# Two of sixteen x tiles transposed through DRAM and VectorE, in a transformer block whose scheduler is set and drawn anew

## The chip, the cores and the metric

The kernel runs on one core of a Trainium2 chip. The core has five engines, each with its own instruction queue that is worked off in order: TensorE (PE) for matmuls, VectorE (DVE), ScalarE (ACT), GpSimd (POOL), and SyncE (SP), which issues the DMAs here. Engines meet only at semaphores. The metric is the device time of one launch in microseconds (us). Before the change it is 519.75 us, the median of three runs (519.67 to 520.14).

## The reference

A pre-norm transformer block on 2048 rows of width 512, in float32: sliding dilated attention with 32 heads of width 16 (each row looks at itself and at 7 rows before it at steps of two), then an MLP of width 1792 with a squared ReLU.

```python
h = x + _A_ref(_layernorm(x), A_wqkv, A_wo)
h2 = h + _B_ref(_layernorm(h), B_w1, B_b1, B_w2, B_b2)
# _A_ref:
qkv = (x @ wqkv).reshape(B, S, 3, H, Dh).transpose(2, 0, 3, 1, 4)
idx = pos[:, None] - (jnp.arange(8) * 2)[None, :]
logits = jnp.where(idx >= 0, einsum("bhsd,bhswd->bhsw", q, kg) * Dh ** -0.5, -1e9)
o = einsum("bhsw,bhswd->bhsd", softmax(logits), vg) @ wo
# _B_ref:
r = relu(h @ w1 + b1); out = (r * r) @ w2 + b2
```

## The kernel before

Matmuls run on a split of every operand into a high half (rounded to the fast matmul type, `fp32r`) and a low half (the rest): three products, high by high, high by low, low by high, give the float32 accuracy. So each operand costs a cast (`hi`, line 322, ACT) and a subtraction (`lo`, line 327, POOL or DVE). In the trace the halves are called xh and xl (of x), oh and ol (of the attention output o), big_h and big_l (of wqkv, later of the normalised h), rh and rl (of the MLP's hidden rows).

The 2048 rows are 16 tiles of 128; four tiles make a unit, u = 0 to 3. The stages:

- **qkv.** Tiles 0 to 3 run first, in pieces of 384 columns (`qkv_first`, product at line 457 with result mm, copied to y by ACT at line 508) while wqkv is still arriving. Its 16 pieces wraw are loaded (line 488), cast (big_h<-wraw) and subtracted one by one. Tiles 4 to 15 run in pairs: `x_chain(t)` (lines 826 to 835) loads x, normalises it on ACT (lines 378 to 390), transposes it and splits it, and `qkv` multiplies. The results go to DRAM (qkv_d).
- **The transpose of x**, two ways. `pe_turn` (line 401) transposes four 128x128 blocks on PE into PSUM (tr); ACT casts xh from there and DVE subtracts xl, and only then is that PSUM buffer free. `turned` (lines 437 to 446) writes the rows to DRAM (t_d), reads them back in another order (back), and DVE transposes 32x32 blocks (`turn`, line 428); then ACT casts and POOL subtracts (`split_turned`). In the kernel before, every x tile takes the first way, and the normalised h of units 1 to 3 the second.
- **Attention**, 16 items (unit u, column group g), lines 548 to 625: DVE multiplies q by a window of k (line 572, pr<-qp,k), sums (line 577), does the softmax with ACT's exponential (line 590), multiplies by v (line 603, pr<-le,v), and POOL adds the window up (line 621), the last of these adds writing o. There are three buffers of pr, so a product on DVE can wait for POOL's last add.
- **Output product and MLP.** `to_mlp(u)` brings o of the unit into transposed form (unit 0 by PE; units 1 to 3 by way of DRAM, DMAs o_d and back, four DVE turns, ACT's oh and POOL's ol), multiplies by wo (`wo_product`, result wo), adds h on DVE (line 332, h<-wo,h), normalises h and turns it by the second way; its halves become big_h and big_l of the unit's MLP. The MLP runs over f = 0 to 13 blocks of 128 hidden columns: a product with w1 (mm), ReLU and square on ACT, the split, and the product with w2 two blocks later, into four accumulators (acc, line 735). The work of the next unit's `to_mlp` is put after block `TO_MLP` of the running unit. Six PSUM buffers serve mm, tr, wo and acc alike: during the MLP four are held by acc and two are left, so a late reader of one (an h addition, a ReLU) stops PE.

The order on every engine is set before the launch by a list scheduler in the kernel itself (`Plan`). Every step has a due time: for PE's steps their place in PE's own list, for the rest the time at which the steps behind it are due, less their durations, an estimated DMA time and a margin (`WAIT`), and no later than a time written in the code, such as `need[u] - ITEM * (G - g) - BEFORE[u]` for attention. To the due time a random number is added (`NOISE`, `SEED`), and each engine takes next, among the steps that are ready, the one with the earliest due time. `AHEAD` limits how early a load may go, `KEEP` and `SPARE` how many row buffers are left for more urgent steps, `W2_EACH` spaces the preparation of w2. SP issues all DMAs in this order, with at most 8 under way.

Of the kernel before, what the change touches and what calls it, by code (L numbers as in the profile page):

```python
# [32 lines left out]
FA = 6  # L33
WARM = 46
ITEM = 18.0
BEFORE = 12, 16, 8, 8
X_BY_PE = True
W2_EACH = 5.5
LO = ("POOL",)
LAGW = 2  # L40
NOISE, SEED = 0.5, 171
LEAD = 10.0
BY_PE = (0,)
TO_MLP = 9
T0 = 8.0

ROWS = {"A": 9, "B": 11, "C": 3}
CLASS = {"x": "A", "o": "B", "h": "B"}
SEM = 0.15
AHEAD = 6.0  # L50
WAIT = {"DVE": 1.2, "ACT": 0.6, "POOL": 1.2, "SP": 0.8}
KEEP = 4
BUSY = 1.1
SPARE = 2

# [20 lines left out]
class Plan:  # L78
# [5 lines left out]
    def add(self, eng, fn, r=(), w=(), by=None, dma=None, ahead=None, first=None,  # L84
            keep=None, lead=0.0):
        t = Task()
        t.n, t.fn, t.by, t.dma, t.ahead = len(self.tasks), fn, by, dma, ahead
        t.keep = keep if keep is not None else KEEP if dma is not None else SPARE
        t.eng = dict(eng)
# [39 lines left out]
    def deadlines(self):  # L129

        draw = random.Random(SEED)
        for t in reversed(self.tasks):
            d = min([s.alap for s in t.succs], default=1e6) - t.dur - t.lat - WAIT.get(t.only, 1.0)
            t.alap = t.pe if t.pe is not None else d if t.by is None else min(d, t.by)
# [110 lines left out]
def block_kernel(ctx, tc, x, wqkv, wo, w1, b1, w2, b2, out):  # L245
# [52 lines left out]
    def buf(tag, shape, dt=F32, name=None):  # L298
        pool = pools.get(tag, att if tag in ("kv", "q", "pr", "o") else work)
        return Buf(tag, lambda: pool.tile(list(shape), dt, name=name or tag, tag=tag,  # L300
                                          bufs=bufs[tag]))

    def row(name, cls, shape=(P, D), dt=F32):
        return buf(cls, shape, dt, name)
# [9 lines left out]
    def pool(us, fn, **k):  # L314
        return plan.add({"POOL": us}, lambda e: fn(), **k)

    def load(count, packet, fn, **k):
        return plan.add({"SP": 0.45 if plan.pe < T0 + 1 else 0.55}, lambda e: fn(nc.sync),
                        dma=dma_us(count, packet), **k)

    def hi(n, dst, src, r, w, **k):
        act(n, lambda: nc.scalar.copy(dst(), src()), r=r, w=w, **k)  # L322
# [15 lines left out]
    def natural(t, by_pe):  # L338
        return t.get() if by_pe else t.get().rearrange("p (a c k) -> p a k c", k=KB, a=KB)

    def blocked(t, by_pe):
        return t.get() if by_pe else t.get().rearrange("p (a k c) -> p a k c", k=KB, a=KB)

    def block(t, k):
        return lambda: t.get().rearrange("p (m k) -> p k m", k=KB)[:, k]
# [26 lines left out]
    def norm_act(src, dst, cls, by_pe):  # L372

        sq, sv = row("sq", cls), buf("sv", (P, 4))

        def sums(e):
            s = sv.get()
            nc.scalar.activation(sq.get(), src.get(), AF.Copy, accum_out=s[:, 0:1])  # L378
            nc.scalar.activation(s[:, 1:2], s[:, 0:1], AF.Copy, scale=-1.0 / D)
            nc.scalar.activation(sq.get(), src.get(), AF.Square, bias=s[:, 1:2],  # L380
                                 accum_out=s[:, 2:3])
            nc.scalar.activation(s[:, 3:4], s[:, 2:3], AF.Copy, scale=1.0 / D, bias=EPS)
        plan.add({"ACT": 2.2}, sums, r=[src], w=[sv, sq])
        pool(0.6, lambda: nc.gpsimd.tensor_tensor(out=sv.get()[:, 0:1], in0=sv.get()[:, 3:4],
                                                  in1=mhalf, op=ALU.pow), r=["mhalf"], w=[sv])

        def apply(e):
            s = sv.get()
            nc.scalar.activation(s[:, 2:3], s[:, 1:2], AF.Copy, scale=s[:, 0:1])
            nc.scalar.activation(blocked(dst, by_pe), natural(src, by_pe), AF.Identity, scale=s[:, 0:1],  # L390
                                 bias=s[:, 2:3])
        plan.add({"ACT": 1.1}, apply, r=[src, sv], w=[dst, sv])


    def pe_turn(srcs, r, **k):

        tr = buf("ps", (P, KB, P), name="tr")

        def go(e):
            for n, s in enumerate(srcs):  # L400
                nc.tensor.transpose(tr.get()[:, n, :], s(), ident)  # L401
        plan.add({"PE": 0.45}, go, r=list(r) + ["ident"], w=[tr], lead=LEAD, **k)
        return tr

    def split(src, name, engs=("POOL", "DVE")):
        h, l = [row(name + p, CLASS[name], (P, KB, P), F32R) for p in "hl"]
        hi(D, h.get, src.get, r=[src], w=[h])
        lo(D, l.get, src.get, h.get, r=[src, h], w=[l], engs=engs)
        return h, l
# [27 lines left out]
    def turned(src, cls):  # L437

        d = Dram(dram.tile([P * D], F32, name="t_d"))
        turn_write(d, src)  # L440
        back, t = row("back", cls), row("turned", cls)
        turn_read(d, back)
        turn(back, t)
        return t

    def split_turned(t, name):
        h, l = [row(name + p, CLASS[name], (P, KB, P), F32R) for p in "hl"]
        hi(D, lambda: by_block(h.get()), lambda: by_row(t), r=[t], w=[h])
        lo(D, lambda: by_block(l.get()), lambda: by_row(t), lambda: by_block(h.get()),
           r=[t, h], w=[l], engs=LO)  # L450
        return h, l
# [17 lines left out]
    def load_x(t, name="xt", **k):  # L469
        b, e, i = where(t)  # L470
        xt = row(name, CLASS[name[0]])
        load(128, 2048, lambda q: q.dma_start(xt.get(), x_v[b, e, i]), w=[xt], **k)
        return xt
# [11 lines left out]
    def load_wqkv(g, k, **more):  # L485
        raw = row("wraw", ("pair", "B", "C", "C")[g], (P, 3, GC))
        src = wqkv.rearrange("(p k) (c n) -> k p c n", k=KB, c=3)[k]
        load(384, 512, lambda q: q.dma_start(raw.get(), src[:, :, g * GC:(g + 1) * GC]), w=[raw],
             ahead=AHEAD if g > 1 else None, **more)
        return raw  # L490
# [136 lines left out]
    def load_h(t, by):  # L627
        return load_x(t, "h", by=by, ahead=AHEAD)

    def split_raw(dst, src_ap, shape, keys, engs=LO, count=128, packet=2048,  # L630
                  by=None):
        raw = row("raw", "C", shape)
        load(count, packet, lambda q: q.dma_start(raw.get(), src_ap), w=[raw], ahead=AHEAD)
        hi(D, lambda: dst(0), raw.get, r=[raw], w=keys[0], by=by)
# [62 lines left out]
    def w2_job(f, by):  # L697
        raw = row("raw2", "C")
        load(128, 2048, lambda q: q.dma_start(raw.get(), w2[f * P:(f + 1) * P, :]), w=[raw],
             ahead=AHEAD)  # L700
        t = buf("pair", (P, 2, D), F32R, "w2s")
        hi(D, lambda: t.get()[:, 0], raw.get, r=[raw], w=[(t, 0)], by=by)
        lo(D, lambda: t.get()[:, 1], raw.get, lambda: t.get()[:, 0], r=[raw, (t, 0)], w=[(t, 1)],
           engs=LO, by=by + 1)
        load(128, 4096, lambda q: q.dma_start(w2_d[f], t.get().bitcast(F32)), r=[(t, 0), (t, 1)],
             w=[("w2d", f)], by=by + 3)

    def get_w2(f):
        t = buf("pair", (P, 2, D), F32R, "w2s")
        load(128, 4096, lambda q: q.dma_start(t.get().bitcast(F32), w2_d[f]), r=[("w2d", f)],  # L710
             w=[(t, 0), (t, 1)], ahead=AHEAD)
        return t
# [16 lines left out]
    def mlp2(f, hid, w2s, acc, js, first, last, split_):  # L729
        rh, rl = hid  # L730

        def run(terms, r, lead, end):
            def go(e):
                for n, (l, wn, j) in enumerate(terms):
                    nc.tensor.matmul(acc[j].get(), l.get()[:, j * P:(j + 1) * P],  # L735
                                     w2s.get()[:, wn], start=lead and n < len(js),
                                     stop=end and n >= len(terms) - len(js))
            plan.add({"PE": len(terms) * 0.23}, go, r=r, w=[acc[j] for j in js])
        one = [(rh, 0, j) for j in js] + [(rh, 1, j) for j in js]
        two = [(rl, 0, j) for j in js]  # L740
        if split_:
            run(one, [rh, (w2s, 0), (w2s, 1)], first, False)
            run(two, [rl, (w2s, 0)], False, last)
        else:
            one.insert(1, two[0])
            run(one, [rh, rl, (w2s, 0), (w2s, 1)], first, last)
# [79 lines left out]
    def x_chain(t):  # L826
        xt = load_x(t, ahead=AHEAD)
        xn = row("xn", "A")
        norm_act(xt, xn, "A", X_BY_PE)
        if X_BY_PE:  # L830
            tr = pe_turn([block(xn, k) for k in range(KB)], [xn])
            xT[t] = split(tr, "x", ("DVE",))
        else:
            xT[t] = split_turned(turned(xn, "A"), "x")
# [5 lines left out]
    def items(u):  # L840
        whole = buf("unit", (P, R, D), name="o") if u in BY_PE else None
        for g in range(G):
            os_[u, g] = item(u, g, need[u] - ITEM * (G - g) - BEFORE[u], whole)

# [15 lines left out]
    for f in range(FB):  # L860
        w2_job(f, 85.0 + W2_EACH * f)

# [48 lines left out]
    for u in range(NU):  # L911
# [5 lines left out]
        for f in range(FB):  # L917
# [4 lines left out]
            if f >= 2:  # L922
# [4 lines left out]
                else:  # L927
                    mlp2(g, hid[g], w2s[g], acc, range(R), g == 0, False, True)
            if not last and f == TO_MLP:
                to_mlp(u + 1, need[u + 1])  # L930
# [66 lines left out]
```

## Time and profile before

| what | value |
|---|---|
| median of three runs | 519.75 us |
| the profiled execution's own time | 518.26 us |
| its span in the trace | 516.5 us |
| granted TensorE clock | 1.00 |
| chain of work that ended last | PE 74%, POOL 10%, ACT 6%, DVE 6% |
| DMA | 126.67 MB, 245 GB/s in the mean |

Times in the views are us from the start of the span, and a row of a timeline reads: start, length, engine, line, operation, result and operands, shape, how many instructions the row joins, and in brackets how long the engine had been idle before and what released it. The ends of matmuls are modelled and overlap the next one's start, so the distance between starts tells more than a matmul's length. A whole qkv stage lasts until about 165 us; the MLPs of units 0 to 3 then take some 90 us each.

### The profile page before, as it was taken

The page shows a single profiled execution, that of the slowest core. Times are in us where ns is not written, and L with a number is a line of the kernel's source. Part 1 is how long each engine was busy: PE and PEld are TensorE (multiplying, and loading weights), DVE is VectorE, ACT ScalarE, POOL GpSimd, SP SyncE. Part 2 cuts the span into 40 slices and gives each one's busy share as a digit, 9 for nine tenths or more (in the row PEclk, how much of TensorE's full clock was granted, in tenths as well). Part 3 has the DMA queues.
Part 4 walks back from the last instruction along what each step waited for, and adds up shares of the span by engine and source line. Part 5 has one row for each costly group of instructions (what it writes and reads, how often), then busy time and mean ns, then how long its engine had stood idle before and what let it go on. Part 6 is the DMA issues. An engine that isn't in the chain of part 4 may idle for free.

```text
span 516.5 us, 6774 instructions
## 1 busy us (share of the span) xinstructions
PE 503.6 (98%) x2308; PEld 420.2 (81%) x2308; DVE 330.3 (64%) x314; ACT 290.8 (56%) x553; POOL 318.0 (62%) x270
## 2 busy tenths in 40 slices
PE   8999899999999999999999999899999999999997
PEld 8989788888888878787788887778887887888885
DVE  6269989898899799975889967684012112445103
ACT  4538977777356364479744476665367745433341
POOL 6321767977876879798796789269844515222210
PEclk9999999999999999999999999999999999999999
DMA  7699588999999976979867847844453732899422
GB/s 211 190 283 337 168 250 296 318 355 400 364 334 301 388 249 208 341 231 340 291 215 247 284 161 242 277 143 139 149 199 106 236 125 89 297 347 355 180 82 81
DMA packets 81489, 126.67 MB, mean 245 GB/s; under 512 B 7216, under 2 KB 48688, under 8 KB 81456
## 3 DMA queue, kind: packets, MB, share of 16 engines
q1 hardware_dynamic: 81312, 126.12, 72.7%
q8 instruction: 18, 0.29, 0.2%
q14 instruction: 15, 0.12, 0.1%
q10 hardware_dynamic: 144, 0.13, 0.1%
HBM read 89.43 MB, written 36.83 MB: 244 GB/s over the span
## 4 chain that ended last, share of the span: by engine, by line
PE 74%; POOL 10%; ACT 6%; DVE 6%; issue 4%; POOLq 0%; ACTq 0%; DVEq 0%
PE mm L457 45%; PE acc L735 21%; POOL pr L621 5%; PE wo L457 5%; ACT big_h L322 2%; PE tr L401 2%; DVE le L577 2%; POOL ol L327 2%; POOL rl L327 1%; PE tr L803 1%; DVE pr L603 1%; DVE pr L572 1%; POOL o L621 1%; ACT sq L380 1%; ACT sq L378 1%
## 5 line engine op out<-in xcount | busy, mean ns | idle before, releaser
L327 POOL TENSOR_TENSOR rl<-r,rh 128x512 fp32r<-128x512 f32 x53 | 68.7, 1297 | 91.9 <-ACT rh L322 89.1
L621 POOL TENSOR_TENSOR pr<-pr 128x1024 f32<-128x1024 f32 (+1 forms) x64 | 117.2, 1853 | 11.8 <-DVE pr L603 11.5
L735 PE MATMUL acc<-w2s,rh 128*128 128x512 f32 x444 | 111.1, 390 | 0.4 <-DMA w2s<-w_d 0.4
L722 ACT ACTIVATE r<-mm,b_sb 128x512 f32<-128x512 f32 x56 | 38.3, 686 | 109.1 <-PE mm L457 108.2
L735 PEld LDWEIGHTS acc<-w2s,rh 128*128 128x128 f32 x444 | 83.2, 188 | 18.5 <-DMA w2s<-w_d 0.8
L572 DVE TENSOR_TENSOR pr<-qp,k 128x2048 f32<-128x2048 f32 x32 | 72.8, 2276 | 19.8 <-POOL o L621 15.1
L603 DVE TENSOR_TENSOR pr<-le,v 128x2048 f32<-128x2048 f32 x32 | 72.3, 2284 | 6.7 <-POOL o L621 6.1
L577 DVE TENSOR_REDUCE le<-pr 128x128 f32<-128x2048 f32 x32 | 73.1, 2284 | 0.8
L735 PE MATMUL acc<-w2s,rl 128*128 128x512 f32 x222 | 60.4, 390 | 0.0
L457 PE MATMUL mm<-big_h,xh 128*128 128x512 f32 (+1 forms) x208 | 50.3, 377 | 2.5 <-DVE xl L327 1.4
L457 PE MATMUL mm<-big_h,xl 128*128 128x512 f32 (+1 forms) x208 | 50.9, 377 | 0.0
L457 PE MATMUL mm<-big_l,xh 128*128 128x512 f32 (+1 forms) x208 | 50.2, 375 | 0.0
L735 PEld LDWEIGHTS acc<-w2s,rl 128*128 128x128 f32 x222 | 41.6, 188 | 9.2 <-DVE rl L327 0.4
L457 PEld LDWEIGHTS mm<-big_h,xh 128*128 128x128 f32 x208 | 37.8, 188 | 9.1 <-DVE xl L327 1.6
L457 PEld LDWEIGHTS mm<-big_l,xh 128*128 128x128 f32 x208 | 37.9, 188 | 5.3
L457 PEld LDWEIGHTS mm<-big_h,xl 128*128 128x128 f32 x208 | 37.8, 188 | 5.2
L428 DVE STREAM_TRANSPOSE turned<-back 128x512 f32<-128x512 f32 x24 | 16.4, 694 | 35.4 <-DMA back<-o_d 18.4
L457 PE MATMUL mm<-big_h 128*128 128x512 f32 x128 | 34.8, 393 | 3.1 <-DVE h L332 2.5
L322 ACT CAST rh<-r 128x512 fp32r<-128x512 f32 x56 | 34.7, 622 | 2.5
L724 ACT ACTIVATE r<-r 128x512 f32<-128x512 f32 x56 | 35.4, 633 | 1.3
L457 PE MATMUL mm<-big_l,big_h 128*128 128x512 f32 x128 | 34.2, 389 | 0.0
L457 PE MATMUL mm<-big_h,big_l 128*128 128x512 f32 x128 | 34.2, 389 | 0.0
(103 smaller groups left out, 787.2 us busy)
## 6 DMA issues: line engine op xcount, KB each, us to landing
w2s<-w_d SPq DMA_DIRECT2D x56, 512.0 KB, 4.7
k<-qkv_d SPq DMA_DIRECT2D x16, 704.0 KB, 6.0
v<-qkv_d SPq DMA_DIRECT2D x16, 704.0 KB, 5.8
qkv_d<-y SPq DMA_DIRECT2D x18, 512.0 KB, 4.5
raw<-in_B_w_dram SPq DMA_DIRECT2D x28, 256.0 KB, 6.3
w_d<-w2s SPq DMA_DIRECT2D x14, 512.0 KB, 5.9
xt<-in_A_x_dram SPq DMA_DIRECT2D x16, 256.0 KB, 5.4
q<-qkv_d SPq DMA_DIRECT2D x16, 256.0 KB, 5.3
```

Source lines behind the costliest of these rows:

```text
L322: act(n, lambda: nc.scalar.copy(dst(), src()), r=r, w=w, **k)
L327: lambda e: engines[e].tensor_tensor(out=dst(), in0=src(), in1=h(), op=ALU.subtract), r=r, w=w, **k)
L401: nc.tensor.transpose(tr.get()[:, n, :], s(), ident)
L428: vec(D, lambda: nc.vector.transpose(dst.get(), src.get()[:, part]), r=[src], w=[dst, *w])
L457: nc.tensor.matmul(ps(), l(), rr(), start=start and i == 0, stop=stop and i == len(terms) - 1)
L572: vec(2048, lambda pr=pr, i0=i0: nc.vector.tensor_tensor(out=pr.get(), in0=qp.get()[:, i0:i0 + IQ].unsqueeze(2).to_broadcast([P, IQ, W, GC ...
L577: vec(2048, lambda pr=pr, i0=i0: nc.vector.tensor_reduce(out=lg()[:, i0:i0 + IQ].rearrange("p i w h -> p (i w h)"), in_=pr.get().rearrange ...
L603: vec(2048, lambda p2=p2, i0=i0: nc.vector.tensor_tensor(out=p2.get(), in1=window(vs.get(), i0, [DH, GH], [1, DH]), op=ALU.mult, in0=ex()[ ...
L621: nc.gpsimd.tensor_tensor(out=dst, in0=a, in1=b_, op=ALU.add)
L722: act(D, lambda: nc.scalar.activation(r.get(), ps.get(), AF.Relu, bias=b1_sb[:, f:f + 1]), 0.08, r=[ps, "b1"], w=[r], keep=2)
L724: act(D, lambda: nc.scalar.activation(r.get(), r.get(), AF.Square), w=[r])
L735: nc.tensor.matmul(acc[j].get(), l.get()[:, j * P:(j + 1) * P], w2s.get()[:, wn], start=lead and n < len(js), stop=end and n >= len(terms) ...
```

## The change

```diff
-BEFORE = 12, 16, 8, 8
-X_BY_PE = True
-W2_EACH = 5.5
+BEFORE = 8, 4, 12, 8
+X_BY_DRAM = (14, 15)
+W2_EACH = 6.0
...
-NOISE, SEED = 0.5, 171
+NOISE, SEED = 0.3, 448
...
-TO_MLP = 9
+TO_MLP = 10
...
-AHEAD = 6.0
-WAIT = {"DVE": 1.2, "ACT": 0.6, "POOL": 1.2, "SP": 0.8}
-KEEP = 4
+AHEAD = 7.0
+WAIT = {"DVE": 1.2, "ACT": 0.6, "POOL": 1.6, "SP": 0.8}
+KEEP = 5
 BUSY = 1.1
-SPARE = 2
+SPARE = 1
...
     def x_chain(t):
         xt = load_x(t, ahead=AHEAD)
         xn = row("xn", "A")
-        norm_act(xt, xn, "A", X_BY_PE)
-        if X_BY_PE:
+        norm_act(xt, xn, "A", t not in X_BY_DRAM)
+        if t not in X_BY_DRAM:
             tr = pe_turn([block(xn, k) for k in range(KB)], [xn])
             xT[t] = split(tr, "x", ("DVE",))
         else:
             xT[t] = split_turned(turned(xn, "A"), "x")
```

Tiles 14 and 15 take the way through DRAM. All other lines are numbers that the scheduler reads, and they move instructions on every engine. The rows below are the order of the instructions on one engine (line, operation, result and operands, shape, repeats), at three places.

**The qkv phase, near 25 to 60 us.** ACT before, around the last casts of wqkv:

```order
L508 ACTIVATE y<-mm,rs 128x384 x2
L322 CAST big_h<-wraw 128x3x128 x2
L508 ACTIVATE y<-mm,rs 128x384 x2
L565 COPY qp<-q 128x512
L322 CAST big_h<-wraw 128x3x128
L508 ACTIVATE y<-mm,rs 128x384 x3
L322 CAST big_h<-wraw 128x3x128
```

and ACT now:

```order
L322 CAST big_h<-wraw 128x3x128 x3
L508 ACTIVATE y<-mm,rs 128x384 x2
L565 COPY qp<-q 128x512
L508 ACTIVATE y<-mm,rs 128x384 x2
L322 CAST big_h<-wraw 128x3x128
L508 ACTIVATE y<-mm,rs 128x384
```

The last cast stands one y copy earlier, and the one before it is done with the others ahead of qp. DVE before, around the second x tile that is split in this phase's pairs:

```order
L595 RECIPROCAL sm<-sm 128x32
L577 TENSOR_REDUCE le<-pr 128x128
L332 TENSOR_TENSOR le<-le,sm 128x256
L332 TENSOR_TENSOR le<-le,mask 128x256
L603 TENSOR_TENSOR pr<-le,v 128x2048 x2
L327 TENSOR_TENSOR xl<-tr,xh 128x512
L585 TENSOR_REDUCE mx<-le 128x32
```

and DVE now:

```order
L595 RECIPROCAL sm<-sm 128x32
L577 TENSOR_REDUCE le<-pr 128x128
L332 TENSOR_TENSOR le<-le,sm 128x256
L327 TENSOR_TENSOR xl<-tr,xh 128x512
L603 TENSOR_TENSOR pr<-le,v 128x2048 x2
L332 TENSOR_TENSOR le<-le,mask 128x256
```

The subtraction xl went ahead of the two products with v.

**The two new turns, near 135 to 145 us.** DVE now, behind the h additions of unit 0 (the rows with back are the new ones; before, two xl<-tr,xh stood in this stretch):

```order
L332 TENSOR_TENSOR h<-wo,h 128x512 x2
L349 BN_STATS st<-h 128x6
L577 TENSOR_REDUCE le<-pr 128x128
L350 BN_AGGR mv<-st 128x2
L349 BN_STATS st<-h 128x6
L428 STREAM_TRANSPOSE turned<-back 128x512
L332 TENSOR_TENSOR le<-le,mask 128x256
L350 BN_AGGR mv<-st 128x2
L585 TENSOR_REDUCE mx<-le 128x32
L428 STREAM_TRANSPOSE turned<-back 128x512
```

Both turns stand in line with the statistics of unit 0's h and with the attention of unit 1.

**Unit 2's output product, near 300 to 325 us.** DVE before:

```order
L428 STREAM_TRANSPOSE turned<-back 128x512
L603 TENSOR_TENSOR pr<-le,v 128x2048
L332 TENSOR_TENSOR h<-wo,h 128x512
L572 TENSOR_TENSOR pr<-qp,k 128x2048
L603 TENSOR_TENSOR pr<-le,v 128x2048
L332 TENSOR_TENSOR h<-wo,h 128x512 x2
L577 TENSOR_REDUCE le<-pr 128x128
L572 TENSOR_TENSOR pr<-qp,k 128x2048
L585 TENSOR_REDUCE mx<-le 128x32
L332 TENSOR_TENSOR h<-wo,h 128x512
```

and DVE now:

```order
L603 TENSOR_TENSOR pr<-le,v 128x2048
L572 TENSOR_TENSOR pr<-qp,k 128x2048
L428 STREAM_TRANSPOSE turned<-back 128x512
L332 TENSOR_TENSOR h<-wo,h 128x512
L603 TENSOR_TENSOR pr<-le,v 128x2048
L577 TENSOR_REDUCE le<-pr 128x128
L332 TENSOR_TENSOR h<-wo,h 128x512
L585 TENSOR_REDUCE mx<-le 128x32
L572 TENSOR_TENSOR pr<-qp,k 128x2048
L332 TENSOR_TENSOR h<-wo,h 128x512
L332 TENSOR_TENSOR le<-le,mx 128x256
L332 TENSOR_TENSOR h<-wo,h 128x512
```

The two products with k moved ahead of the first and of the third addition; the additions stand singly.

## The prediction

> **What bounds the kernel now.** First I read the page's busy shares, then TensorE's (PE's) waits, then PE's timeline where those waits fall.
>
> ```profile
> PE 503.6 (98%) x2308; PEld 420.2 (81%) x2308; DVE 330.3 (64%) x314; ACT 290.8 (56%) x553; POOL 318.0 (62%) x270
> ```
>
> PE is busy for 503.6 of 516.5 us; no other engine passes two thirds. So only two things move the end: matmuls that PE no longer issues, and moments in which PE stands still. The second kind is small, and the view of PE's waits names it (what it waited for, us in total, times, longest):
>
> ```profile
> PE mm L457 <- ACT big_h L322: 2.7, 3, 1.1
> PE mm L457 <- DVE h L332: 2.5, 1, 2.5
> PE mm L457 <- DVE xl L327: 1.4, 1, 1.4
> ...
> PE wo L457 <- DVE h L332: 0.5, 1, 0.5
> PE acc L735 <- DMA w2s<-w_d: 0.4, 1, 0.4
> ```
>
> That is 7.5 us. A new order of instructions can take no more than about this from the time, and it can add any amount. PE's timeline shows where the stalls lie (start, length, ..., idle time before and its releaser):
>
> ```profile
> 36.63 1.68 PE L457 MATMUL mm<-big_h,xh 128*128 128x384 f32 x8 [1.13 <-ACT big_h L322]
> ...
> 59.16 1.19 PE L457 MATMUL mm<-big_h,xh 128*128 128x512 f32 x4 [1.37 <-DVE xl L327]
> ...
> 315.51 1.20 PE L457 MATMUL wo<-wo_h,oh 128*128 128x512 f32 x4 [0.49 <-DVE h L332]
> ...
> 324.67 1.21 PE L457 MATMUL mm<-big_h 128*128 128x512 f32 x4 [2.52 <-DVE h L332]
> ...
> 344.76 1.19 PE L457 MATMUL mm<-big_h,w1a_h 128*128 128x512 f32 x4 [0.71 <-ACT big_h L322]
> ...
> 432.71 1.20 PE L457 MATMUL mm<-big_h,w1a_h 128*128 128x512 f32 x4 [0.88 <-ACT big_h L322]
> ```
>
> The reader is to see three places: the qkv products (36 and 59 us), the output products of unit 2 (315 to 325 us), and the handovers from one unit's MLP to the next (345 and 433 us). I go through the change by these places.
>
> **The transposes.** Tiles 14 and 15 leave PE: eight 128x128 transposes. What four of them cost is seen where a group of four stands between groups of four matmuls:
>
> ```profile
> 52.17 0.63 PE L401 MATMUL tr<-ident,xn 128*128 128x128 f32 x4
> 52.56 1.18 PE L457 MATMUL mm<-big_l,xh 128*128 128x512 f32 x4
> 53.57 1.08 PE L457 MATMUL mm<-big_h,xl 128*128 128x512 f32 x4
> 54.49 1.07 PE L457 MATMUL mm<-big_h,xh 128*128 128x512 f32 x4
> ```
>
> From the transposes' start to the start of the group after next are 53.57 - 52.17 = 1.40 us; one group of four matmuls takes 54.49 - 53.57 = 0.92, so the four transposes take 0.48 and the eight 0.96, say **1.0 us**. The Trainium skill ("VectorE: DVE Perf Modes", The three transpose paths) gives 390 ns for one 128x128 transpose on TensorE (bf16), by which eight would be worth 3.1 us as an estimate; the rows above show 0.12 us each in a stream, and the measurement decides.
>
> What the two tiles need instead, by groups of the forms that units 1 to 3 already run (busy us, mean ns), and the two DMAs (KB, median us to landing):
>
> ```profile
> L390 ACT ACTIVATE hn<-h,sv 128x512 f32<-128x512 f32 x12 | 15.7, 1307 | 0.4
> L322 ACT CAST oh<-turned 128x512 fp32r<-128x512 f32 x12 | 13.1, 1128 | 8.1 <-POOL ol L327 5.6 <-DVE turned L428 2.5
> ...
> L390 ACT ACTIVATE xn<-xt,sv 128x512 f32<-128x512 f32 x12 | 9.8, 816 | 0.4
> L322 ACT CAST xh<-tr 128x512 fp32r<-128x512 f32 x16 | 9.4, 586 | 4.2 <-PE tr L401 4.0
> ```
>
> ```profile
> L327 POOL TENSOR_TENSOR ol<-turned,oh 128x512 fp32r<-128x512 f32 x12 | 18.7, 1565 | 2.9 <-ACT oh L322 2.8
> ```
>
> ```profile
> t_d<-hn SPq DMA_DIRECT2D x12, 256.0 KB, 3.7
> back<-t_d SPq DMA_DIRECT2D x12, 256.0 KB, 4.3
> ```
>
> Each tile: ACT +0.49 (norm) and +0.54 (cast), together 2.1 us for two; VectorE (DVE) a turn of 0.7 in place of a subtraction of 0.7, so nothing; GpSimd (POOL) two new subtractions, 3.1 us; SP four more DMAs. From the norm to the cast half it is 1.3 + 3.7 + 4.3 + 0.7 + 1.1 = 11.1 us, against a PE turn and a cast. The tile's x is loaded long before, so this hides if VectorE reaches its turn in time. In the new order the first turn stands behind the fourth h addition and two statistics of unit 0, which puts it at about 140 us (my estimate from those rows' times before, 137 us, less what PE gains early); the cast is done near 143. PE wants tile 14 at about 143.5. I cost it at nothing. If it is late, PE waits one for one, and the attention steps that are queued behind the turn on DVE wait as well; I allow 1 us for that.
>
> **The qkv products.** At 36 us PE waits for the last cast of wqkv, which ACT ran late:
>
> ```profile
> 35.60 0.58 ACT L508 ACTIVATE y<-mm,rs 128x384 f32<-128x384 f32 x1 [1.56 <-PE mm L457]
> 36.08 0.50 ACT L322 CAST big_h<-wraw 128x384 fp32r<-128x384 f32 x1
> ```
>
> It stood behind a y copy that itself waited 1.56 us for a product of PE, and its load was issued late on SP, among the loads of the first attention item. In the new order that load leaves SP earlier and the last cast stands one y copy ahead. The 1.13 us should go; at worst the load lands as late as before and most of it stays. At 59 us PE waits for an xl half, since with it a PSUM buffer comes free:
>
> ```profile
> 54.01 4.49 DVE L603 TENSOR_TENSOR pr<-le,v 128x2048 f32<-128x2048 f32 x2
> 58.42 0.68 DVE L327 TENSOR_TENSOR xl<-tr,xh 128x512 fp32r<-128x512 f32 x1
> ```
>
> Now the subtraction stands ahead of the two products of 4.49 us, so it can run near 54 us and the 1.37 us go. What is late next is the pair of products, by 0.7 us, which only attention needs. Early gain: 1.13 + 1.37 = **2.5 us**.
>
> **What the early gain runs into.** Attention does not get faster, and unit 1's output product depends on it. The chain of its last quarter (POOL's last sum, DVE's turn, ACT's cast) and the product:
>
> ```profile
> 203.41 0.77 POOL L621 TENSOR_TENSOR o<-pr 128x256 f32<-128x256 f32 x1
> ```
>
> ```profile
> 217.70 0.70 DVE L428 STREAM_TRANSPOSE turned<-back 128x512 f32<-128x512 f32 x1
> ```
>
> ```profile
> 218.44 1.12 ACT L322 CAST oh<-turned 128x512 fp32r<-128x512 f32 x1 [2.24 <-DVE turned L428]
> ```
>
> ```profile
> 221.30 1.98 PE L457 MATMUL wo<-wo_h,oh 128*128 128x512 f32 x8
> ```
>
> The cast is done at 219.56, so there were 1.74 us to spare. PE would now be there at 221.3 - 2.5 - 0.4 (the w2s load of that place goes out ahead of the o write on SP) = 218.4, as the eight transposes are made up by other matmuls that stand ahead of this product. With the chain unmoved it waits until about 219.6: **1.2 us are given back**. The chain's ends: 1 us earlier (POOL's longer list is absorbed by its idle 38%), or later by POOL's new work, which ahead of that sum is 4.2 us longer by my count of the order (two new subtractions and other halves moved there). I take it unmoved, as POOL waited for DVE just ahead of that stretch. Up to here: 1.0 + 2.5 + 0.4 - 1.2 = 2.7 us.
>
> **Unit 2's h additions.** The 3.0 us at 315 and 325 us come from DVE's in-order queue:
>
> ```profile
> 310.37 2.29 DVE L572 TENSOR_TENSOR pr<-qp,k 128x2048 f32<-128x2048 f32 x1 [4.01 <-POOL o L621]
> 312.58 2.28 DVE L603 TENSOR_TENSOR pr<-le,v 128x2048 f32<-128x2048 f32 x1
> 314.77 1.28 DVE L332 TENSOR_TENSOR h<-wo,h 128x512 f32<-128x512 f32 x2
> ...
> 321.40 2.29 DVE L572 TENSOR_TENSOR pr<-qp,k 128x2048 f32<-128x2048 f32 x1 [3.15 <-POOL o L621]
> 323.61 0.41 DVE L585 TENSOR_REDUCE mx<-le 128x32 f32<-128x256 f32 x1
> 323.94 0.68 DVE L332 TENSOR_TENSOR h<-wo,h 128x512 f32<-128x512 f32 x1
> ```
>
> The additions stand behind products that wait for POOL to free a buffer. TO_MLP = 10 puts unit 2's output products one block later, 4.5 to 7.2 us of PE work by the order, and by then those waits are mostly over. But the same two products now stand ahead of the first and the third addition: on before's POOL times the first would run near 313.5 where PE wants its buffer near 312, and the third near 324. I keep 1.1 us of stall: **1.9 us gone**, between nothing and 3.0.
>
> **The handovers.** One more block between unit 2's h and the next unit covers the cast that was 0.71 late, though h itself is later; I take 0.5 of it. Unit 3's 0.88 keeps its structure: nothing.
>
> **Sum.** 2.7 + 1.9 + 0.5 = 5.1 us off the profiled execution's own 518.26 us, so 513.2. That execution lies 1.5 under the median of 519.75, so on the median's scale **514.7 us**. A measurement of this kernel can tell about 0.2%, 1.0 us, from no change.
>
> **The rivals.**
> - *Everything goes*: attention keeps up at unit 1 and no addition is late: 1.0 + 2.5 + 0.4 + 3.0 + 0.7 = 7.6, so 512.2. For it: POOL and DVE have idle time. Against it: only 1.74 us to spare at unit 1. Chance 0.13.
> - *Attention takes it back*: unit 1's product starts near 222, after which only the 1.9 + 0.5 of unit 2 and little else stay: about 2.6, so 517.1. For it: DVE is nine tenths busy in most slices up to 210 us. Chance 0.18.
> - *The stalls only move*: the new draw makes as many waits elsewhere, and the transposes' 1.0 is left: 518.8, the same within what can be told. That the change does not do what it says is excluded for the transposes, since the new order has eight fewer. Chance 0.10.
> - *Slower: POOL's list*. If the 4.2 us show whole at unit 1's last sum, its product starts at 219.6 + 4.2 = 223.8 instead of 221.3, and unit 2's additions, which wait for the same engine, keep their 3.0: 2.5 lost, less 0.9 of PE work done ahead, so +1.6 and 521.4. It decides once that sum ends after about 206.7 instead of 204.2. Chance 0.12. The Trainium skill ("SBUF — State Buffer", SBUF: two separate sides) speaks for it: a DVE operation with two SBUF inputs and a GpSimd operation that reads SBUF lock each other out for a whole instruction, so that each new POOL subtraction could meet a 2.28 us product. The trace doesn't bear it out: the product at 312.58 above took its usual 2.28 beside this POOL addition, whose form takes 2408 ns in the mean:
>
> ```profile
> 312.24 2.40 POOL L621 TENSOR_TENSOR pr<-pr 128x1024 f32<-128x1024 f32 x1
> ```
>
> **How the numbers follow.** My forecast has 0.47, with a range of its own of 513 to 516.8 (h additions 0 to 3.0, chain 1 us either way). Faster: 0.47 + 0.13 + 0.18 = 0.78; same 0.10; slower 0.12. The range of 512.0 to 519.0 takes in all but the slower rival and the tails.
>
> **What would show it.** Right: no PE idle time over 0.5 us between 30 and 65 us; 56 transposes of xn in place of 64; PE's first product of unit 1 waits about 1 us for ACT's oh at 219 to 220; h additions of unit 2 leave PE at most 1.5 us of stall. Wrong: a wait of PE at 141 to 146 us for tile 14's cast, a sum of POOL for unit 1 that ends after 206, or the last wqkv cast still after 35.5 us.

## The result and the profile after

| | before | after |
|---|---|---|
| median (lowest to highest, six runs each) | 519.71 us (519.15 to 520.14) | 515.15 us (513.04 to 515.94) |
| the profiled execution's own time | 518.26 us | 514.67 us |
| its span | 516.5 us | 512.9 us |
| PE's idle time in its list of waits, without the wait for ident at the start | 8.1 us | 5.7 us |

The ratio is 0.991, with a 95% interval of 0.989 to 0.993: faster by 0.9%. The forecast was 514.7 us. Of the executions behind this section and the experiments, three took over 1.5% longer than the fastest of their kernel (526.57 us in xl_late, 522.03 in o_first, 518.85 in o_first_act); medians and ranges keep them, ratios and intervals leave them out, and o_first_act's trace, which is one of them, is not read.

The busy shares after, from the first part of the page:

```profile
PE 501.9 (98%) x2300; PEld 419.2 (82%) x2300; DVE 333.6 (65%) x314; ACT 292.0 (57%) x552; POOL 323.0 (63%) x273
```

PE is still the bound, with eight matmul instructions fewer, and POOL has worked 5.0 us more. PE's waits of the changed kernel (waited for; us in total, times, longest):

```profile
PE mm L457 <- DVE big_l L327: 2.0, 1, 2.0
PE wo L457 <- ACT oh L322: 1.9, 2, 1.2
PE tr L803 <- POOL ident masks.py:199: 1.3, 1, 1.3
PE mm L457 <- ACT big_h L322: 0.9, 1, 0.9
PE tr L401 <- ACT y L534: 0.4, 1, 0.4
PE mm L457 <- ACT r L722: 0.3, 1, 0.3
PE wo L457 <- ACT r L722: 0.2, 1, 0.2
```

The waits for h, for xl, for w2s and for two of the three casts big_h are gone. Four entries are new: one wait for a subtraction big_l, two for oh, and two small ones for a copy y and for a ReLU ahead of an output product. Leaving out ident, the list fell by 8.1 - 5.7 = 2.4 us; with the transposes' 1.0 that is 3.4 of the 3.6 us by which the span shrank. PE's timeline has the larger new waits at these places (start, length, operation, and in brackets the idle time before and its releaser):

```profile
58.40 0.75 PE L401 MATMUL tr<-ident,xn 128*128 128x128 f32 x4 [0.40 <-ACT y L534]
...
166.26 1.20 PE L457 MATMUL mm<-big_h,w1a_h 128*128 128x512 f32 x4 [2.04 <-DVE big_l L327]
...
220.75 1.20 PE L457 MATMUL wo<-wo_h,oh 128*128 128x512 f32 x4 [0.70 <-ACT oh L322]
...
308.03 1.20 PE L457 MATMUL wo<-wo_h,oh 128*128 128x512 f32 x4 [1.24 <-ACT oh L322]
```

Ahead of the last of them DVE's turn waited for a DMA, the read back of o:

```profile
306.12 0.71 DVE L428 STREAM_TRANSPOSE turned<-back 128x512 f32<-128x512 f32 x1 [1.99 <-DMA back<-o_d]
```

The largest, 2.04 us ahead of 166.26, lies where unit 0's MLP begins, and no step of the prediction has it. To see where it comes from, read two timelines of the changed kernel backwards from there. First DVE's:

```profile
144.11 2.25 DVE L572 TENSOR_TENSOR pr<-qp,k 128x2048 f32<-128x2048 f32 x1
...
149.10 0.34 DVE L595 RECIPROCAL sm<-sm 128x32 f32<-128x32 f32 x1
153.13 2.29 DVE L572 TENSOR_TENSOR pr<-qp,k 128x2048 f32<-128x2048 f32 x1 [3.69 <-POOL o L621]
...
158.13 4.49 DVE L603 TENSOR_TENSOR pr<-le,v 128x2048 f32<-128x2048 f32 x2
162.65 0.43 DVE L332 TENSOR_TENSOR le<-le,mask 128x256 f32<-128x256 f32 x1
162.99 2.28 DVE L572 TENSOR_TENSOR pr<-qp,k 128x2048 f32<-128x2048 f32 x1
165.19 0.41 DVE L585 TENSOR_REDUCE mx<-le 128x32 f32<-128x256 f32 x1
165.52 0.68 DVE L327 TENSOR_TENSOR big_l<-tr,big_h 128x512 fp32r<-128x512 f32 x1
```

The subtraction at 165.52 frees the PSUM buffer that PE wants. It stands in DVE's queue behind attention products, and the first of those waited 3.69 us, until 153.13, for POOL to write an o. Now POOL's timeline:

```profile
144.20 1.60 POOL L327 TENSOR_TENSOR xl<-turned,xh 128x512 fp32r<-128x512 f32 x1
145.75 1.30 POOL L621 TENSOR_TENSOR pr<-pr 128x512 f32<-128x512 f32 x1
147.01 1.56 POOL L327 TENSOR_TENSOR xl<-turned,xh 128x512 fp32r<-128x512 f32 x1
...
151.10 1.29 POOL L621 TENSOR_TENSOR pr<-pr 128x512 f32<-128x512 f32 x1
152.35 0.75 POOL L621 TENSOR_TENSOR o<-pr 128x256 f32<-128x256 f32 x1
```

The two rows xl<-turned,xh are the new subtractions of tiles 14 and 15, 3.2 us in all, and the o for which DVE waits stands behind both. So the trace suggests a chain: new work on POOL, a later o, a hole on DVE, a later big_l, a stall of PE. A timeline shows only who released whom; whether PE's time would fall if a link went has to be tried.

### The profile page after: what moved, and what is told of

Same layout as the page of the kernel before. It is cut to its first block, busy times and chain, and to the rows that moved or that the text cites. A ratio compares the mean times of both kernels' runs of the same rounds, so it can differ in the third digit from the quotient of the medians.

```text
span 512.9 us, 6775 instructions
## 1 busy us (share of the span) xinstructions
PE 501.9 (98%) x2300; PEld 419.2 (82%) x2300; DVE 333.6 (65%) x314; ACT 292.0 (57%) x552; POOL 323.0 (63%) x273
## 4 chain that ended last, share of the span: by engine, by line
PE 72%; DMA 8%; ACT 6%; POOL 5%; DVE 4%; issue 3%; SPq 1%; POOLq 0%; ACTq 0%; DVEq 0%
PE mm L457 41%; PE acc L735 20%; PE wo L457 7%; POOL pr L621 3%; DMA k<-qkv_d 3%; DVE pr L572 2%; PE tr L401 2%; DMA back<-o_d 2%; PE tr L803 1%; DMA qkv_d<-y 1%; DMA xt<-in_A_x_dram 1%; DMA o_d<-o 1%; POOL rl L327 1%; ACT r L722 1%; ACT big_h L322 1%
## 5 line engine op out<-in xcount | busy, mean ns | idle before, releaser
L621 POOL TENSOR_TENSOR pr<-pr 128x1024 f32<-128x1024 f32 (+1 forms) x64 | 118.8, 1883 | 11.7 <-DVE pr L603 8.4
L428 DVE STREAM_TRANSPOSE turned<-back 128x512 f32<-128x512 f32 x26 | 17.8, 696 | 36.6 <-DMA back<-o_d 24.1
```

Source lines behind the costliest of these rows:

```text
L428: vec(D, lambda: nc.vector.transpose(dst.get(), src.get()[:, part]), r=[src], w=[dst, *w])
L621: nc.gpsimd.tensor_tensor(out=dst, in0=a, in1=b_, op=ALU.add)
```

## The experiments

In each run "before" is the kernel before, timed on the same chip beside the others of its group: 519.44 us in the first group (again, xl_late, bigl_early, x_by_pe), 519.50 in the second (no_xl_pool, x_only, sched_only, before_h_early), 519.06 in the third (o_first, o_first_act, draw_171, draw_449). Ratios are to that.

Planning anew moves hundreds of instructions. Most of the kernels below therefore keep an order that was planned already and move single instructions within one engine's list; all other engines keep theirs. The lines for it stand in `kernel`, between the planning and the loop that issues the order:

```python
...                            # relink() is left out here
lanes = {e: [t for t in plan.order if t.on == e] for e in ("PE", "DVE", "ACT", "POOL", "SP")}
was = {e: list(l) for e, l in lanes.items()}
def move(e, n, before):        # instruction n of engine e goes ahead of instruction `before`
    t, b = was[e][n], was[e][before]
    lanes[e].remove(t)
    lanes[e].insert(lanes[e].index(b), t)
plan.order = relink(lanes)     # one order in which each engine's list is kept
```

**again.** The changed kernel itself, as the measure for the other three of its group.

> The changed kernel itself, beside the others on one chip: 514 to 516 us, with PE's waits of 2.0 us at 164 (for DVE's big_l), 0.9 in two pieces at 220 and 223, 1.2 at 308 and 0.9 at 428.

Median 514.19 us (513.12 to 516.19), ratio 0.990 [0.987, 0.993].

**xl_late: is the early gain given back?** The prediction let part of the qkv gain be lost at unit 1, because attention would not move. Here the xl half goes back behind the two products, as it stood before:

```diff
+    move("DVE", 35, 38)
```

> The changed kernel's order with one step put back: the subtraction xl of the second tile of the pairs stands behind the two v products again. Theory A (what PE gains in the qkv phase is given back further on, where it waits for attention): PE waits about 1.4 us again at 58, the wait at 164 shrinks by as much to 0.6 or so, and the time is that of the changed kernel within 0.5 us. Theory B (the early gain is kept to the end): 1.4 us more than the changed kernel.

Median 516.02 us (515.03 to 526.57), ratio 0.994 [0.992, 0.996]: 1.8 us more than again. The stall at 59 us is back, and PE's timeline shows that the one behind it kept its size and came some 3.3 us later than in the profile of the result:

```profile
58.78 1.62 PE L457 MATMUL mm<-big_h,xl 128*128 128x512 f32 x4 [2.09 <-DVE xl L327]
...
169.61 1.19 PE L457 MATMUL mm<-big_h,w1a_h 128*128 128x512 f32 x4 [2.03 <-DVE big_l L327]
```

(Not all of the 3.3 us is the moved half: this execution also waited 0.60 us for the last cast at 36 us, and its granted clock was 0.50 from 60 to 62 us.) On DVE the two products at 158.13 moved to 161.48 likewise. Had attention been unmoved, the wait at 166 would have shrunk by what PE came later. Attention is fed by PE through qkv and moves with it, so an early gain is kept.

**bigl_early: is the stall at 166 us real time?** Unit 0's four subtractions big_l go ahead of attention work on DVE. Of the first of them the new place is the one ahead of the product that waited 3.69 us.

```diff
+    move("DVE", 127, 119)
+    move("DVE", 129, 124)
+    move("DVE", 131, 124)
+    move("DVE", 130, 125)
```

> The changed kernel's order with DVE's four subtractions big_l of unit 0 moved up, the first ahead of the product with k that stands at 153 and the others directly behind the two products with v at 158. Both theories: the wait of 2.0 us at 164 goes. Theory A: the wait at unit 1's output product grows from 0.9 to about 2.9 and the time stays within 0.5 us. Theory B: 2 us less than the changed kernel.

Median 512.82 us (511.69 to 513.05), ratio 0.987 [0.984, 0.989]: 1.4 us less than again. The stall at 166 is gone, though attention on DVE is no earlier: DVE now waits for ACT's big_h at that place, and the product behind it starts at 153.46 where it was 153.13.

```profile
152.78 0.69 DVE L327 TENSOR_TENSOR big_l<-tr,big_h 128x512 fp32r<-128x512 f32 x1 [3.00 <-ACT big_h L322]
153.46 2.29 DVE L572 TENSOR_TENSOR pr<-qp,k 128x2048 f32<-128x2048 f32 x1
```

Two small waits came in exchange, 0.29 us for w2s at 182 and 0.59 for big_h at 253, but the wait for oh at unit 1 did not grow:

```profile
219.46 1.21 PE L457 MATMUL wo<-wo_h,oh 128*128 128x512 f32 x4 [0.40 <-ACT oh L322]
```

The oh that PE waits for came some 1.3 us earlier than in the changed kernel (219.46 against 220.75), though POOL's last sum of the unit did not (206.12 against 205.66). The way led over ACT. DVE's turn for this oh stands behind attention work that starts with a softmax sum, and that sum waited for ACT's exponential. In the changed kernel, and then in bigl_early:

```profile
203.30 0.37 ACT L590 ACTIVATE le<-le 128x256 f32<-128x256 f32 x1
```

```profile
202.30 0.36 ACT L590 ACTIVATE le<-le 128x256 f32<-128x256 f32 x1
```

The exponential stands in ACT's queue behind a ReLU of unit 0's MLP (201.38 against 200.39), and that ReLU behind PE's product (199.94 against 198.95). From the sum on (203.70 against 202.70) DVE has no wait up to the turn but one of 0.21 us for a DMA, in the changed kernel (218.83 against 217.54). So a stall of PE at the start of the MLP came back at unit 1 by way of the MLP's own ReLU.

**x_by_pe: what is the way through DRAM worth?** In the changed kernel's order, tiles 14 and 15 are transposed on PE again: both ahead of PE's product at about 140 us, ACT casts from PSUM, DVE subtracts in the place of its turns, and POOL's two subtractions and the four DMAs are gone.

```diff
-        norm_act(xt, xn, "A", t not in X_BY_DRAM)
+        norm_act(xt, xn, "A", True)
...
+                nc.tensor.transpose(tr.get()[:, k, :], block(xn, k)(), ident)
...
+        lanes["PE"].insert(lanes["PE"].index(was["PE"][207]), new)
+        lanes["POOL"].remove(lo_)
+        lanes["DVE"].insert(lanes["DVE"].index(was["DVE"][(112, 113)[n_]]), lo_)
```

> The changed kernel's order with tiles 14 and 15 transposed on PE again, at the same place (both turns ahead of the product that starts at 140, xl on DVE where the second turn stood, no xl on POOL, no DMAs for them). Theory A: PE pays 1.0 us there, but POOL has 3.1 us less ahead of the sum for which DVE's product waits 3.7 us at 149; that wait shrinks to about 0.6, the wait of 2.0 at 164 goes, attention reaches unit 1's product about 2 us earlier and the waits at 220 go: time 0.5 to 2 us less than the changed kernel. Theory B (the way through DRAM hides, and is worth the eight transposes): 1.0 us more.

Median 511.05 us (510.54 to 512.32), ratio 0.984 [0.981, 0.987]: 3.1 us **less** than again, with 1.0 us more of transposes on PE (from their start at 138.11 to the start of the second group behind them at 140.92, less 1.82 for the group of eight in between). In this order, the part of the change that takes work off the bounding engine makes the kernel slower. DVE's hole shrank from 3.69 to 2.60 us and ended 1.6 us earlier:

```profile
151.55 2.29 DVE L572 TENSOR_TENSOR pr<-qp,k 128x2048 f32<-128x2048 f32 x1 [2.60 <-POOL o L621]
```

PE, later by its 1.0 us of transposes, then waits for no big_l, and the wait for oh at 308 us is gone too.

**no_xl_pool: POOL's 3 us, or another part of that way?** The way through DRAM stays, with its DMAs, DVE turns and casts, but the two subtractions on POOL are left out. The products read the high half in the place of the low one, so the low halves of these two tiles are missing from the result and the high ones enter once more. (`dram_way` holds the steps of a tile's way through DRAM; step 4 is POOL's subtraction.)

```diff
+    for tile_ in X_BY_DRAM:
+        lanes["POOL"].remove(dram_way[tile_][1][4])
+        xT[tile_][1].get = xT[tile_][0].get
```

> The changed kernel's order; tiles 14 and 15 still go through DRAM, but POOL's two subtractions xl for them are left out and the products with xl read xh instead (so the low half of these two tiles is left out and their high half counted twice). Theory C (the price of the way through DRAM is POOL's 3.1 us at 144 to 149): DVE's wait for POOL's o at 149 falls from 3.7 to about 0.6, the wait of 2.0 at 164 goes, and the time is that of the run with both tiles on PE, 511.0, or up to 1.0 less. Theory D (the price is that of the DMAs on SP and of DVE's turns): the wait at 149 and the one at 164 stay, 514 to 515.

Median 510.31 us (509.57 to 511.67), ratio 0.982 [0.979, 0.985]: about 3.9 us under again, across two groups whose befores differ by 0.06. So two instructions of 1.6 us on an engine that is busy for 63% of the span cost about their whole length (3.9 against 3.2 us, a difference within the scatter of the runs), and the rest of the way through DRAM costs little. DVE's product now waits 1.44 us and starts at 149.67 instead of 153.13:

```profile
149.67 2.29 DVE L572 TENSOR_TENSOR pr<-qp,k 128x2048 f32<-128x2048 f32 x1 [1.44 <-POOL o L621]
```

So not the whole hole of 3.69 us comes from the two subtractions: 1.44 us of it are left without them, and 2.60 in x_by_pe. What is left is POOL's other work ahead of that o and its wait for a cast of w2 on ACT (0.73 us, and 1.78 in x_by_pe).

**o_first: amount of work, or order?** POOL does all it does in the changed kernel, but the add that writes o goes ahead of the second xl, and also of what stood between that xl and it: three small steps of a normalisation, a subtraction for w2 and another add.

```diff
+    move("POOL", 82, 78)
```

> The changed kernel's order with one instruction moved: on POOL, the last add of the half item for which DVE waits 3.7 us at 149 goes directly behind the add that it needs, ahead of the second x tile's subtraction xl, a normalisation step, a w2 subtraction and another add. Theory C (what the way through DRAM cost was the place of POOL's subtractions in its queue): DVE's wait at 149 falls under 0.5, the wait of 2.0 at 164 goes, time 510 to 511.5, 3 to 4 under the changed kernel, with both tiles still through DRAM. Theory G (POOL's total work counts, not its order): DVE waits as long a little later, 513.5 to 515.

Median 511.79 us (510.03 to 522.03), ratio 0.985 [0.982, 0.988]: 2.4 us less than again, across two groups whose befores differ by 0.38. That is a little more than was expected at the top of the first case (511.5), and its interval just touches that of again. One moved instruction gives more than half of what no_xl_pool gave. POOL's rows:

```profile
143.43 1.58 POOL L327 TENSOR_TENSOR xl<-turned,xh 128x512 fp32r<-128x512 f32 x1
144.94 1.31 POOL L621 TENSOR_TENSOR pr<-pr 128x512 f32<-128x512 f32 x1
146.33 0.76 POOL L621 TENSOR_TENSOR o<-pr 128x256 f32<-128x256 f32 x1
147.04 1.56 POOL L327 TENSOR_TENSOR xl<-turned,xh 128x512 fp32r<-128x512 f32 x1
```

and the product on DVE that waits for no one:

```profile
148.57 2.23 DVE L572 TENSOR_TENSOR pr<-qp,k 128x2048 f32<-128x2048 f32 x1
```

In PE's waits big_l is gone, and oh fell from 1.9 to 0.4 us in all, with none left at 308:

```profile
PE tr L803 <- POOL ident masks.py:199: 1.3, 1, 1.3
PE mm L457 <- ACT big_h L322: 0.9, 1, 0.9
PE wo L457 <- ACT oh L322: 0.4, 1, 0.4
PE mm L457 <- ACT r L722: 0.3, 1, 0.3
PE tr L401 <- ACT xn L390: 0.3, 1, 0.3
PE wo L457 <- ACT r L722: 0.2, 1, 0.2
```

This kernel computes all that the reference does and is faster than both kernels of the case. Order alone was enough to end DVE's wait. But the o comes 6.0 us earlier here (done at 147.09 against 153.10), more than the one subtraction of 1.56 us that it passed, so the run doesn't price that subtraction by itself.

**o_first_act.** The same, with two steps moved up on ACT: the copy y that PE waits for at 58 us, and the ReLU that PE waits for at 223 us, ahead of one of unit 1's output products.

```diff
+    move("ACT", 50, 47)
+    move("ACT", 203, 200)
```

> As the run with POOL's add moved, and two moves on ACT: the copy y that PE waits for at 58 goes ahead of the next tile's sums, which wait for a DMA there, and the ReLU for which PE waits 0.2 at 223 goes ahead of the w1 cast before it. Both PE waits go, 0.5 to 0.9 less than the run with POOL's add moved alone; if attention holds PE at 220 anyway, nothing.

Median 511.19 us (510.58 to 518.85), ratio 0.983 [0.982, 0.985]. Its interval overlaps that of o_first, so the two cannot be told apart.

**before_h_early: unit 2's additions by themselves.** In the order of the kernel before, two of unit 2's h additions go ahead of the attention work on DVE that held them up. Nothing else is changed.

```diff
+    move("DVE", 237, 236)
+    move("DVE", 241, 239)
```

> The order of the kernel before with two h additions of unit 2 moved up on DVE: the second stands ahead of the product with v (row 314.77 before), the fourth ahead of the product with k that waits for POOL (321.40 before). Theory E (PE's 3.0 us at 315 and 325 come from DVE's in-order queue and are kept when it is cured): PE's waits for h fall under 0.5 and the time is 516.5 to 517.5. Theory F (what is gained there is given back at the next handovers, where hn is late): waits for big_h grow by 1 us or more, and the time is 518.5 to 519.5.

Median 515.92 us (514.90 to 518.04), ratio 0.993 [0.990, 0.996]. The 2.52 us at 325 us are gone from PE's timeline and nothing took their place; the 0.5 at 315 stay:

```profile
315.89 1.20 PE L457 MATMUL wo<-wo_h,oh 128*128 128x512 f32 x4 [0.50 <-DVE h L332]
```

Two moved instructions give 3.6 us in the medians and 2.7 in the spans (516.5 to 513.8), most of what the whole change gives. The medians gain more than the stall's length and more than was expected (516.5 to 517.5); the last section has a likely part of it.

**x_only and sched_only: the two parts planned anew.** x_only has the settings and the draw of before and sends tiles 14 and 15 through DRAM; sched_only has the new settings and draw and sends none. In both the scheduler plans the whole order again.

Against the kernel before, x_only has

```diff
-X_BY_PE = True
+X_BY_DRAM = (14, 15)
```

and against the changed kernel, sched_only has

```diff
-X_BY_DRAM = (14, 15)
+X_BY_DRAM = ()
```

> The kernel before, with its own settings and draw, and tiles 14 and 15 through DRAM; the order is planned anew. Theory C (the way through DRAM costs POOL more than it saves on PE, and the gain of the change is that of the settings and the draw): no gain over the kernel before, 518.5 to 522. Theory B (it hides): 518.5 or less, one us under the kernel before.

> The changed kernel's settings and draw, with all sixteen tiles on PE; the order is planned anew, so its stalls are others. Theory C: as good as the changed kernel or better, 511 to 515. Theory B: 1 us more than the changed kernel, 515 to 516.

x_only: 531.0 us (529.96 to 531.97), ratio 1.021 [1.018, 1.024]. sched_only: 521.27 us (519.39 to 523.51), ratio 1.003 [1.001, 1.005]. Both are slower than before, and the change that joins them is faster: the two effects do not add, since each run is also another order. What was expected was missed for both runs, by either theory: x_only was to take 522 at most, and sched_only 516, as x_by_pe (the same work in the frozen order) takes 511.05. In x_only five of PE's waits, besides the first for ident, are over 1.6 us. sched_only's two largest are of a size that neither kernel of the case has:

```profile
PE mm L457 <- ACT big_h L322: 5.3, 3, 3.5
PE wo L457 <- ACT oh L322: 3.3, 1, 3.3
```

**draw_171 and draw_449: how much is the draw?** The changed kernel with another seed of the random numbers, and no other edit; here that of draw_171, and draw_449 has 449 in its place.

```diff
-NOISE, SEED = 0.3, 448
+NOISE, SEED = 0.3, 171
```

> The changed kernel with the draw of the kernel before (seed 171) and nothing else changed; planned anew. If the draw decides most of the change: anywhere from 512 to 530, with other stalls of PE. If the settings decide: 514 to 516.

> The changed kernel with the next seed, 449, and nothing else changed; planned anew. The same two cases: 512 to 530 if the draw decides, 514 to 516 if the settings do.

draw_171: 518.12 us (516.80 to 518.91), ratio 0.998 [0.996, 0.999]. draw_449: 520.13 us (519.31 to 520.53), ratio 1.001 [1.000, 1.003]. With the same settings and the same way of the two tiles, three draws give 515, 518 and 520 us, a spread as large as the change's whole effect. PE's longest wait in draw_449 is again one of its own, in the qkv stage:

```profile
PE mm L457 <- ACT big_h L322: 3.4, 4, 0.9
PE mm L457 <- ACT xh L322: 2.8, 1, 2.8
PE mm L457 <- DVE xl L327: 1.7, 2, 1.5
```

So the 0.9% belongs to this order, with its seed; it is not what the new settings or the way through DRAM give by themselves. How the old settings scatter under other seeds was not run.

## Why the prediction came out right, and where it did not

The time was 0.45 us above the forecast and inside the likeliest case's own range. That it came so near is in part luck: a stall that was not foreseen and a shift between the two scales of the sum cancel. Step by step:

- **The bound.** PE at 98% before and after, and a gain of the size of the stalls that went: right. (The 7.5 us of the prediction were the rows it showed; two waits for a ReLU, 0.6 us, make the 8.1 of the table.) In every kernel of the frozen orders the medians moved the way PE's list of waits did.
- **The transposes.** Eight went (2308 to 2300 instructions), worth 1.0 us as said, which x_by_pe shows again. That the way through DRAM "costs nothing" is the step that **failed**. The prediction looked for the wrong lateness: it asked whether tile 14's halves come in time for PE, and they did, with no wait at 141 to 146 us. It wrote down POOL's 3.1 us, and let POOL's idle 38% absorb it. But an in-order queue absorbs work only if nobody waits for what stands behind it, and an o did. What the runs show in place of nothing is some 4 us in this order: 3.9 by no_xl_pool, and by x_by_pe 3.1 net of the transposes, 4.1 with them. o_first gets 2.4 of it back with the way through DRAM kept.
- **The qkv products.** 2.5 us were to go. The stall at 36 us is gone, as is the one at 59; 0.40 for another y copy is left at 58. The first is gone by a narrow margin, since xl_late, with the same order up to there, waited 0.60 at 36. So about 2.1, and xl_late puts the second of them at 1.8 us of the time.
- **"1.2 us are given back" at unit 1.** PE does wait there, 0.70 + 0.21 us, near the time that was named. But the reason given, an attention chain that stays where it was, **fell**: in xl_late PE came later, and the chain with it. POOL's last sum of the unit started 2.2 us later than before (205.66 against 203.41) and ended at 206.4, past the 206 that the prediction set as its own sign of error. PE itself came at 220.05 instead of 218.4, chiefly for the stall at 166. The size was near for a reason that was not right: with bigl_early's trace, the chain runs over PE's own MLP and ACT, not over POOL's sum alone.
- **Unit 2's h additions.** 1.9 of 3.0 us were to go. All 3.0 went: no wait for h is in the list, and before_h_early shows that such a stall is time. But 1.24 us for oh appeared at 308 us, just ahead of them, so the net is 1.8. It came of a DMA for which DVE's turn waited (the row at 306.12). PE's wait is gone in x_by_pe, no_xl_pool and o_first, and in bigl_early too, where DVE's product still starts at 153.46. So it went wherever the stall at 166 went, and does not hang on the hole at 149 by itself; by what way, no run shows.
- **The handovers.** 0.5 of 0.71 was to go at unit 2, and all of it went; unit 3 kept its wait (0.88 before, 0.87 after): right.
- **The sum.** 5.1 us were forecast between the two profiled executions, and 3.6 came. The missing 1.5 us lie in the 2.04 at 166 us, which the sum did not have. That the median came nearer is scale: before's profiled execution lay 1.5 us under its median, after's 0.5 under its own, so the medians differ by 4.6.
- **The rivals.** "Everything goes", 512.2, is near what o_first reaches with POOL's order changed. The slower rival named the right engine and the right new work, but put its effect at unit 1, where it decides past 206.7; the cost came at unit 0's handover instead, where a wait of DVE passed it on. The rule of the Trainium skill that was named with it ("SBUF — State Buffer", SBUF: two separate sides) does not show: the new subtraction at 144.20 took 1.60 us beside DVE's product at 144.11, which took 2.25, and that form took 1565 ns in the mean before.

What stays open: by what way the wait at 308 us goes with the stall at 166, and the 1.5 us by which o_first stays above no_xl_pool in the medians, across two groups.

## What to carry to other kernels

Work that is moved to an engine with idle time is not free by that engine's busy share: find its place in the in-order queue, name the next instruction behind it for which another engine waits, and follow that wait through to the engine that bounds; here 3.1 us of work for a POOL that was idle for over a third of the span cost some 4 us of the whole, more than the transposes it saved. Where a seed sets the order, compare several draws, or freeze the order, before a gain is put down to a setting. And once PE's list of waits names the late instruction, moving that one ahead in the finished order is cheap and can give as much as a new plan: two instructions gave 0.7% in the order of the kernel before, and one gave 0.5% in that of the changed kernel.

## What the runs showed of the hardware

A stall of PE can cost more than its length, and not in every execution. The changed kernel's stall of 2.04 us was profiled twice. In the run again, PE's timeline behind it reads

```profile
165.16 1.86 PE L457 MATMUL mm<-big_h,w1a_h 128*128 128x512 f32 x4 [2.04 <-DVE big_l L327]
166.81 2.95 PE L457 MATMUL mm<-big_h,w1a_l 128*128 128x512 f32 x8
```

so four matmuls took 166.81 - 165.16 = 1.65 us. In the profile of the result, the same four took 1.03, from the row at 166.26 above to this one:

```profile
167.29 1.99 PE L457 MATMUL mm<-big_h,w1a_l 128*128 128x512 f32 x8
```

The view by stretches gives the granted clock behind the stall (stretch, its length, busy time of PE, PEld, DVE, ACT and POOL with counts, granted clock, DMA share, GB/s), for again:

```profile
165.00:169.00 4.00, 3.84 (x10) 3.03 (x11) 4.00 (x6) 1.42 (x3) 4.00 (x4) 0.57 1.01 390
```

and for the changed kernel's first profile:

```profile
166.00:170.00 4.00, 3.74 (x16) 3.11 (x17) 4.00 (x6) 1.42 (x3) 4.00 (x4) 1.00 1.04 410
```

0.57 against 1.00 over the 4 us behind the same stall, 10 matmuls against 16. Taken one by one, the slower matmuls start 427 ns apart, the others 226 to 236. The Trainium skill ("TensorE: Matmul & The Clock Gate", Part 1: The HAM clock gate) says that TensorE falls to half its clock after an idle window of about 3.4 us, that the window runs freely, and that start to start is then 426.7 ns at N = 512. The spacing agrees with the trace; the length does not, since 2.04 us were enough in one execution, while 2.04 in another and the 2.52 of before's profiled execution were not. The lower clock was also seen behind xl_late's 2.09 us (0.50 from 60 to 62 us) and behind both long stalls of sched_only, 3.53 and 3.26 us (0.57 from 255 to 259, 0.50 from 307 to 310).

Part of the scatter between executions goes with it. Again's mean clock over the whole span was 0.997, which is what some 3 us at half the clock give (an estimate: 0.003 x 513.6 / 0.5 = 3.1). Of the 53 executions of the kernel before in the three groups, the 31 with a mean clock of 0.999 or 1.000 took 518.9 us in the mean, and the 22 with 0.993 to 0.997 took 520.4. Of the changed kernel's twelve (result and again) seven lay at 0.995 to 0.997. bigl_early, x_by_pe and o_first, with no stall over 1 us behind the first transposes, have 0.999 or 1.000 in all thirteen executions that their ratios count, before_h_early is lower in one of six, and sched_only has 0.992 to 0.997 in all ten. So some of what it gains to remove a stall of 2 us or more is likely the clock. This is a correlation: no run held the clock fixed.
